# Transposing the keys and queries of batches 2 to 7 on VectorE in 32x32 blocks, in a fused top-k attention and feed-forward kernel

## The chip, the cores and the metric

The kernel runs on one core of a Trainium2 chip. The metric is the device time of one execution in microseconds (us). Three executions of the kernel before took 1657.47, 1657.69 and 1659.72 us; the median is 1657.69 us.

## The reference

Inputs are q, k and v of 8 batches, 8 heads, 576 tokens and 64 dimensions per head, all f32, and two weight matrices, 512x2048 and 2048x512, which arrive as 64-bit floats and are turned into f32 inside the kernel.

```
scores = scale * np.matmul(q, k.transpose(0, 1, 3, 2))
kth    = np.partition(scores, -32, axis=-1)[..., -32:-31]
scores = np.where(scores >= kth, scores, -1e9)
attn   = softmax(scores)                 # exp, divided by the row's sum
x      = matmul(attn, v), heads side by side   # 4608 rows of 512
h      = x @ w_in
out    = np.where(h > 0, h, exp(min(h, 0)) - 1) @ w_out
```

So each query row keeps its 32 largest of 576 scores; then 4608 rows go through a feed-forward block with the ELU function.

## The kernel before, in words

**Steps.** The attention is cut into 144 steps, 18 a batch. A step takes 128 queries of one pair of heads (the last 64 queries of a batch are shared out as steps that take two pairs of heads). Two heads of 64 dimensions fill the 128 partitions that a matmul sums over. The program is written out in one order by hand, step by step, and every engine runs its part of it in that order.

**What one step does.** TensorE makes the scores of two heads (`scores`, L322) two to three steps ahead; ScalarE copies them to SBUF (L342). VectorE finds the 32nd largest of each row in four rounds: `first_max` takes the eight largest of each head's row (L347), and `next_max` three times strikes the found ones out (`match_replace`, L353) and takes the next eight (L359). GpSimd makes the mask and applies it (L371 to L373), ScalarE takes the exponential and the row sums (L409). TensorE turns the result (`trans`, L449 and L467), ScalarE copies it out of PSUM (L454), and TensorE multiplies it with v (`attend`, L482). When all heads of a group of queries are done, `sums` has VectorE invert the row sums (L418 to L420) and sends them through DRAM to be spread over the partitions (L424, L436), and GpSimd scales the rows (`normalise`, L497).

**Keys and queries.** The scores need q and k with the head dimension on the partitions. For each batch and pair of heads, `load_qk` brings k and q into SBUF with tokens on the partitions (L228, L234), `transpose_qk` turns them: eight 128x128 and two 64-row transposes on TensorE into PSUM (L273, L281), and two ScalarE copies into a `kq` tile of 128 x 2 x 576 (L268). `keep_kq` writes the tile to DRAM (L296), and `load_kq` brings it back for each step that uses it (L302). `kq` tiles come from a ring of five (L95), the tiles that k and q are loaded into from a ring of two (L94). A table `turns` (L652) says at which step a pair is turned. There are four pairs of heads a batch, counted 0 to 31 over the batches: pairs 4 to 7 are turned in steps 2 to 5, pairs 8 to 12 in steps 7 to 11, and pairs 13 to 31 in every second step from 13 to 49. From step 6 on, steps with `transpose_qk` do it right after the scores (L721), and then issue the next pair's load. `load_kq` for steps n+3 and n+4 is issued at the head of an odd step n (L658).

**Feed-forward work.** Blocks of one to three groups of 128 rows become ready as groups are normalised. A block is a list of pieces: `hidden` (x times w_in, L517, then ELU on ScalarE and GpSimd, L531 to L534) and `project` (times w_out, L541, copied and stored, L550 and L553). `feed` is called twice a step and puts pieces into TensorE's order until the step's share is spent; even steps get two 0.3 parts of the share and odd steps two 0.7 parts. The share is what is left by the next due time, at most 6.0 in steps 0 to 71 and 7.2 after (L580); a unit of it stands for about a microsecond of TensorE. What is left after the last step is put out at the end.

**Queues.** All loads and stores but a few at the start are issued by SP, in program order; an issue whose data or buffer isn't ready holds up all behind it. In the first eight steps the weights are loaded and decoded, partly by VectorE.

Of the kernel before, what the change touches and what calls it, by code (L numbers as in the profile page):

```python
# [10 lines left out]
FP32 = mybir.dt.float32  # L11
# [50 lines left out]
def kernel(  # L62
# [9 lines left out]
    nc = tc.nc  # L72
    P = nc.NUM_PARTITIONS
    B, H, S, D = q.shape
    dm, dff = moe_w_in.shape[0], moe_w_in.shape[1] // 2
    J = S // P
    JP = J * P
    R = S - JP
    HS = S // 2
    NHP = H // 2  # L80
# [9 lines left out]
    def pool(name, bufs, **kw):  # L90
        return ctx.enter_context(tc.tile_pool(name=name, bufs=bufs, **kw))

    const = pool("const", 1)
    ldpool = pool("ld", 2)  # L94
    kqpool = pool("kq", 5)  # L95
# [115 lines left out]
    loaded, kqT, kept, vE = {}, {}, {}, {}  # L211

    def load_qk(b, hp):

        first = b == 0 and hp < 2
        aside = (b, hp) in ((0, 1), (0, 2))
        if aside:
            home = xtpool.tile([P, 2, NC * T // 2], FP32, tag="xT", name="kqin")
            home = home[:, :, 0 : (J + 1) * 2 * D].rearrange(
                "p n (j h d) -> p n j h d", j=J + 1, h=2  # L220
            )
        for n, (name, src) in enumerate((("k", k), ("q", q))):
            queue = nc.scalar if first and name == "q" else nc.sync
            if aside:
                t = home[:, n]
            else:
                t = ldpool.tile([P, J + 1, 2, D], FP32, tag="in", name=name + "in")
            queue.dma_start(  # L228
                t[:, 0:J, :, :],
                src[b, 2 * hp : 2 * hp + 2, 0:JP, :].rearrange(  # L230
                    "h (p j) d -> p j h d", j=J
                ),
            )
            queue.dma_start(  # L234
                t[0:R, J, :, :],
                src[b, 2 * hp : 2 * hp + 2, JP:S, :].rearrange("h p d -> p h d"),
            )
            loaded[b, hp, name] = t

    def load_v(b, hp):  # L240

# [56 lines left out]
    def load_kq(u):  # L298
        u.kq = {}
        for hp in u.hps:  # L300
            u.kq[hp] = kqpool.tile([P, 2, S], FP32, tag="kq", name="kq")
            nc.sync.dma_start(u.kq[hp][:], kept[u.g.b, hp][:])  # L302
# [271 lines left out]
    def feed(n, part):  # L574

        left = sum(piece[0] for piece in ffn)
        until = next(r for r in dues if r > n) - n
        share = min(left / until, 6.0 if n < NS // 2 else 7.2)  # L580

        work = 0.0
        for blk in order:
            mine = [piece[0] for piece in ffn if piece[3] is blk]
            work += sum(mine)
            late = work - 1.75 * 8 * blk.n
            if mine and late > 0 and blk.over is not None:
                share = max(share, late / max(blk.over.filled - n, 0.5))
        owed[0] = min(owed[0] + part * share, 8.0)
        while ffn and owed[0] > ffn[0][0] / 2 and ffn[0][2] < decoded[0]:  # L590
            t, piece = ffn.pop(0)[:2]
            piece()
            owed[0] -= t


    EARLY = 6
    sizes = {0: (1, 1, 1, 1, 1, 1, 1, 2), 2: (2, 2, 2, 3), B - 2: (3, 3, 2, 1)}
    steps, first, order = [], {}, []
    for b in range(B):
# [4 lines left out]
        for qt in (0, 1, 2, 3, 4) if b % 2 == 0 else (4, 0, 1, 2, 3):  # L604
            r0 = b * S + (JP if qt == J else qt)
            if qt == J:
# [3 lines left out]
                c0, n = slot * P + (b % 2) * R, R  # L610
                rows = slice(r0, r0 + R)
            else:
                blk, slot = places.pop(0)
                c0, n = slot * P, P
                rows = slice(r0, r0 + J * (P - 1) + 1, J)
            g = Tokens(b, qt, rows, blk, slice(c0, c0 + n))
# [11 lines left out]
    NS = len(steps)  # L628
    dues = [blk.ready for blk in order] + [NS + 5]

    def sums(u):
        u.summed = True
        invert(u.g)
# [3 lines left out]
        if place in ((2, 3, 4, 5, 6) if n in (4, 5) else (3, 4, 5, 6)):  # L637
            weight_slot()

    todo, turns = {}, {}  # L640

    def at(step, fn, *args):
        todo.setdefault(step, []).append((fn, args))
# [2 lines left out]


    for p, pair in enumerate(pairs):
        if p >= NHP:
            n = p - 2 if p < NHP + 4 else p - 1  # L650
            n = n if n < EARLY + 5 else EARLY + 5 + 2 * (n - EARLY - 5)
            turns[n] = pair  # L652
            at(n + 1, keep_kq, *pair)
        elif p >= 2:
            at(p - 1, keep_kq, *pair)

    for u in steps[EARLY + 2 :]:
        at(u.n // 2 * 2 - 3, load_kq, u)  # L658
    for hp in range(1, NHP):
        at(hp, load_v, 0, hp)  # L660
    for b in range(1, B):
# [5 lines left out]
    def load_next():  # L667
        if coming:
            load_qk(*coming.pop(0))

    with tc.manual_schedule():
        load_qk(0, 0)
        nc.scalar.activation(rec[:], rec[:], AF.Copy)
        for hp in (1, 2):
            load_qk(0, hp)
        load_weights(3)
        warm(16)
        for hp in range(2):
            transpose_qk(0, hp, shared=hp == 0)
            steps[hp].kq = {hp: kqT[0, hp]}  # L680
            scores(steps[hp], 0)
            scores(steps[hp], 1, nc.vector.tensor_copy if hp == 0 else nc.scalar.copy)
            if hp == 0:
                load_qk(0, 3)
        load_weights()
        load_v(0, 0)
        first_max(steps[0])
        weight_slot()
        weight_slot()
        for hp in range(2):  # L690
            keep_kq(0, hp)
        for n in range(NS + 4):
            early = n < EARLY
            now, last, done = (
                steps[n + d] if 0 <= n + d < NS else None for d in (0, -1, -2)
            )
            for fn, args in todo.pop(n, []):
                fn(*args)
            gone = None
            if early:  # L700
                if n + 2 < NHP:
                    transpose_qk(0, n + 2)
                ahead = steps[n + 2]
                ahead.kq = {hp: kqT[0, hp] for hp in ahead.hps}
                for half in range(2):
                    scores(ahead, half)
                if n < EARLY - 1:
                    warm(24)
            elif n % 2 == 0:

                for d in (2, 3):
                    if n + d < NS:
                        for half in range(2):
                            scores(steps[n + d], half)
                    if d == 2:
                        for u in steps[n - 4 : n - 2]:
                            if not u.attended:
                                attend(u)
                                gone = u
            if n in turns and not early:  # L720
                transpose_qk(*turns[n])  # L721
                load_next()
            if now and n > 0:
                first_max(now)
            if last and n > EARLY:
                biases(last, early)
                mask(last, 0)
            if early:
                decode(n, 0)
                feed(n, 0.5)  # L730
                if last:
                    exp(last, 0)
                    exp(last, 1)
                next_max(now, (n, 1))
                decode(n, 2)
                if last:
                    trans(last)
                feed(n, 0.5)
                if last and last.ends:
                    sums(last)  # L740
                next_max(now, (n, 3))
                decode(n, 4)
                if last:
                    attend(last)
                if n in turns:
                    transpose_qk(*turns[n])
                if n < EARLY - 1:
                    warm(24)
                next_max(now, (n, 5))
                if last and last.ends:  # L750
                    normalise(last.g)
                mask_early(now)
                decode(n, 6)
                if n >= NHP - 3:
                    load_next()
                continue
            decode(n, 0)
            feed(n, (0.3, 0.7)[n % 2])
            if now:
                next_max(now, (n, 1))  # L760
            decode(n, 2)
            if last:
                if n > EARLY:
                    mask(last, 1)
                exp(last, 0)
            if done and not done.turned:
                trans(done)
            if now:
                next_max(now, (n, 3))
            decode(n, 4)  # L770
            if gone and gone.ends:
                normalise(gone.g)
            feed(n, (0.3, 0.7)[n % 2])
            if now:
                next_max(now, (n, 5))
            decode(n, 6)
            if last:
                exp(last, 1)
            if done and done.ends and not done.summed:
                sums(done)  # L780
        while ffn:
            ffn.pop(0)[1]()

# [32 lines left out]
```

## Time and profile before

| what | us |
|---|---|
| median of three runs | 1657.69 |
| the profiled execution | 1660.85 |
| its span, first to last instruction | 1659.0 |
| TensorE busy | 1593.8 |
| VectorE busy | 1460.3 |
| GpSimd busy | 1141.9 |
| ScalarE busy | 925.5 |

The profile is of one execution. PE is TensorE's matmul and PEld its weight load, which overlaps it, DVE is VectorE, ACT is ScalarE, POOL is GpSimd, SP is SyncE, which only issues transfers. Matmuls are pipelined: a row's mean duration is longer than the distance from one matmul to the next, and the same holds, by less, for VectorE. An f32 product shows as two matmul records and a transpose as one. A group row reads: line, engine, operation, out<-in with shapes, count | busy us, mean ns of one | idle time of the engine before them and what ended it.

### The profile page before, as it was taken

What the parts mean: (1) busy time and instruction counts of PE and PEld (TensorE: products, weight loads), DVE (VectorE), ACT (ScalarE), POOL (GpSimd) and SP (SyncE); (2) the same over time, 40 slices, a digit from 0 to 9 for tenths busy, and PEclk for the clock granted to TensorE, in tenths of its full rate; (3) what the DMA queues carried; (4) which work ended last, traced back from release to release, by engine and by line L of the source; (5) the groups of instructions that cost most, each with busy time, mean ns of one, the idle gap of its engine ahead of it and who ended that gap; (6) DMA issues with size and microseconds to landing.
All of it is one profiled execution on the core that took longest, in us unless ns stands there. A gap on an engine that the chain in (4) does not pass through costs nothing.

```text
span 1659.0 us, 28820 instructions
## 1 busy us (share of the span) xinstructions
PE 1593.8 (96%) x10048; PEld 1074.0 (65%) x10048; DVE 1460.3 (88%) x3074; ACT 925.5 (56%) x1889; POOL 1141.9 (69%) x1456
## 2 busy tenths in 40 slices
PE   6868999999999999999999999999999999999999
PEld 5765877777776776757566566566565566566565
DVE  6999999999999999999999989979989989987000
ACT  5875565656666565646466475466466466455121
POOL 3677777777777786868678678668668668668021
PEclk8879999999999999999999999999999999999999
DMA  9864555444543513121212321221212322210000
GB/s 304 266 184 120 185 186 152 141 132 134 162 141 97 187 52 104 65 88 67 85 71 102 116 83 61 77 85 65 91 70 100 113 68 82 77 42 7 26 7 13
DMA packets 138962, 174.53 MB, mean 105 GB/s; under 512 B 94272, under 2 KB 102464, under 8 KB 138816
## 3 DMA queue, kind: packets, MB, share of 16 engines
q1 hardware_dynamic: 136448, 172.09, 32.3%
q8 instruction: 80, 1.31, 0.3%
q10 hardware_dynamic: 2368, 0.59, 0.2%
q14 instruction: 66, 0.54, 0.1%
HBM read 144.18 MB, written 28.46 MB: 104 GB/s over the span
## 4 chain that ended last, share of the span: by engine, by line
PE 59%; DVE 26%; POOL 5%; issue 4%; DMA 3%; ACT 2%; SPq 1%; POOLq 0%; ACTq 0%
PE ops L541 21%; PE hps L517 19%; DVE m L359 11%; DVE wk L353 11%; PE avps L482 6%; PE scps L322 6%; PE eps L449 4%; DVE m L347 2%; POOL sc L373 1%; POOL gT L534 1%; DMA kin<-in_k_dram 1%; DMA w_out<-in_moe_w_in_dram 1%; POOL wk L371 1%; PE qkps L273 1%; POOL wk L372 1%
## 5 line engine op out<-in xcount | busy, mean ns | idle before, releaser
L359 DVE MAX8 m<-wk 128x8 f32<-128x576 f32 x864 | 609.8, 748 | 0.0
L517 PE MATMUL hps<-xT,w_in 128*128 128x128 f32 (+2 forms) x2432 | 534.6, 375 | 10.4 <-ACT gT L532 5.7
L541 PE MATMUL ops<-w_out,gT 128*128 128x512 f32 x1152 | 519.6, 597 | 7.6 <-ACT osb L550 7.6
L517 PEld LDWEIGHTS hps<-xT,w_in 128*128 128x128 f32 x2432 | 385.0, 194 | 134.8 <-issue 18.5
L353 DVE MATCH_REPLACE8 wk<-m,wk 128x576 f32<-128x576 f32 x576 | 423.6, 744 | 0.0
L373 POOL TENSOR_TENSOR sc<-sc,wk 128x576 f32<-128x576 f32 x276 | 389.2, 1410 | 23.0
L541 PEld LDWEIGHTS ops<-w_out,gT 128*128 128x128 f32 x1152 | 209.9, 190 | 240.2 <-issue 214.2
L409 ACT ACTIVATE sc<-sc,neg 128x576 f32<-128x576 f32 x288 | 224.1, 778 | 229.6 <-POOL sc L373 228.8
L534 POOL TENSOR_TENSOR gT<-gT,n 128x384 f32<-128x384 f32 (+1 forms) x168 | 187.2, 1121 | 189.7 <-ACT n L533 187.0
L371 POOL TENSOR_SCALAR wk<-sc,nth 128x576 f32<-128x576 f32 x276 | 206.2, 747 | 26.9
L353 DVE MATCH_REPLACE8 wk<-m,sc 128x576 f32<-128x576 f32 x288 | 211.8, 744 | 0.0
L342 ACT COPY sc<-scps 128x576 f32<-128x576 f32 x287 | 168.9, 639 | 75.6 <-PE scps L322 73.6
L322 PE MATMUL scps<-kq 64*128 64x288 f32 (+3 forms) x1344 | 181.3, 419 | 23.7 <-ACT sc L342 9.9
L347 DVE MAX8 m<-sc 128x8 f32<-128x576 f32 x288 | 201.3, 741 | 0.3
L372 POOL TENSOR_SCALAR wk<-wk 128x576 f32<-128x576 f32 x276 | 184.0, 667 | 22.8
L454 ACT COPY et<-eps 128x1024 f32<-128x1024 f32 x144 | 144.5, 1004 | 96.3 <-PE eps L449 95.3
L482 PE MATMUL avps<-et,vE 128*64 128x128 f32 (+1 forms) x3200 | 176.3, 265 | 5.6 <-ACT et L454 3.3
L482 PEld LDWEIGHTS avps<-et,vE 128*64 128x64 f32 x3200 | 158.7, 137 | 32.1 <-issue 24.7
L449 PEld LDWEIGHTS eps<-ident,sc 128*128 128x128 f32 x1152 | 134.1, 141 | 54.2 <-issue 36.6
L322 PEld LDWEIGHTS scps<-kq 64*128 64x128 f32 (+1 forms) x1344 | 101.5, 175 | 93.3 <-issue 31.2
L449 PE MATMUL eps<-ident,sc 128*128 128x128 f32 x1152 | 151.1, 274 | 7.3 <-ACT sc L409 4.6
L531 ACT ACTIVATE n<-hps 128x384 f32<-128x384 f32 (+1 forms) x168 | 90.2, 537 | 114.0 <-PE hps L517 105.4
(71 smaller groups left out, 1001.3 us busy)
## 6 DMA issues: line engine op xcount, KB each, us to landing
kq<-kqd SPq DMA_DIRECT2D x152, 576.0 KB
kqd<-kq SPq DMA_DIRECT2D x32, 576.0 KB
rb<-recd SPq DMA_DIRECT2D x64, 128.0 KB
out_dram<-osb SPq DMA_DIRECT2D x32, 256.0 KB
kin<-in_k_dram SPq DMA_DIRECT2D x30, 256.0 KB
qin<-in_q_dram SPq DMA_DIRECT2D x29, 256.0 KB
w_out<-in_moe_w_in_dram SPq DMA_DIRECT2D x2, 2048.0 KB
vE<-in_v_dram SPq DMA_DIRECT2D x32, 128.0 KB
```

The costliest lines, as they stand in the source:

```text
L322: nc.tensor.matmul(ps[rows, j, at : at + keys.stop - keys.start], u.kq[hp][r, 1, q0 : q0 + g.ql], u.kq[hp][r, 0, keys], start=True, stop=True,
L347: nc.vector.max(u.m1[:, i, :], u.sc[:, i, :])
L353: nc.vector.match_replace(u.wk[:, i, :], u.m[:, i, :], u.cur[:, i, :], TAKEN)
L359: nc.vector.max(u.m[:, i, :], u.cur[:, i, :])
L371: nc.gpsimd.tensor_scalar(pen, s, u.nth[:, i : i + 1], 2.0**100, ALU.add, ALU.mult)
L373: nc.gpsimd.tensor_tensor(s, s, pen, ALU.add)
L409: nc.scalar.activation(s, s, AF.Exp, bias=u.neg[:, i : i + 1], scale=scale, accum_out=g.den[:, at : at + 1],)
L449: nc.tensor.transpose(ps[:, i, c * P : (c + 1) * P], e[:, k0 + c * P : k0 + (c + 1) * P], ident[:],)
L482: nc.tensor.matmul(g.av[r, hp, 0:ql], vE[g.b, hp][:, i, (c + i) % (J + 1), :], u.et[:, at, q0 : q0 + ql], start=(c == 0), stop=(c == J),)
L517: nc.tensor.matmul(ps[:, f % G, :], w_in[:, i, f * P : (f + 1) * P], blk.xT[:, i, 0:N], start=(i == 0), stop=(i == NC - 1),)
L534: nc.gpsimd.tensor_tensor(g, g, n, ALU.subtract)
L541: nc.tensor.matmul(blk.o[:], blk.gT[f // NG][:, f % NG, s * P : (s + 1) * P], w_out[:, f, :], start=(f == 0), stop=(f == NF - 1),)
```

## The change

Three things change.

1. `turns` keeps only pairs 4 to 7. Pairs 8 to 31 (batches 2 to 7) are loaded by a new `load_blocks` and turned by a new `transpose_blocks`, pair 8+j at the end of step 13+4j, the last in step 105. The new load puts 32 tokens by 32 dimensions blocks where VectorE's transpose wants them: partitions 32·part to 32·part+31 hold tokens, `part` names the head and half of its dimensions, and the free axis runs over token groups and 32 dimensions. It is four main and four remainder transfers for k, and as many for q, with runs of 32 f32. k is issued in step n-3 and q in step n-1, for a transpose in step n. One VectorE instruction of 128x576 turns k and one turns q, straight into the `kq` tile.
2. `load_kq` for steps n+4 and n+5 is issued in even step n, behind the scores.
3. The cap on the feed-forward share is 6.6 in place of 6.0 in steps 0 to 71.

```diff
+    def load_blocks(b, hp, name):
+        t = ldpool.tile([P, J + 1, 2, D], FP32, tag="in", name=name + "bl")
+        t = t[:].rearrange("p j h d -> p (j h d)")[:, 0:S]
+        main = t[:, 0:JP].rearrange("p (c g d) -> p c g d", c=J, d=32)
+        rem = t[:, JP:S].rearrange("p (g d) -> p g d", d=32)
+        for part in range(4):
+            rows = slice(32 * part, 32 * part + 32)
+            h, d0 = 2 * hp + part // 2, part % 2 * 32
+            src = (k if name == "k" else q)[b, h, :, d0 : d0 + 32]
+            nc.sync.dma_start(
+                main[rows], src[0:JP].rearrange("(g i c) d -> i c g d", i=32, c=J)
+            )
+            nc.sync.dma_start(
+                rem[rows], src[JP:S].rearrange("(g i) d -> i g d", i=32)
+            )
+        loaded[b, hp, name] = t
+
+    def transpose_blocks(b, hp):
+        t = kqT[b, hp] = kqpool.tile([P, 2, S], FP32, tag="kq", name="kq")
+        for n, name in enumerate("kq"):
+            nc.vector.transpose(t[:, n, :], loaded.pop((b, hp, name)))
...
-        share = min(left / until, 6.0 if n < NS // 2 else 7.2)
+        share = min(left / until, 6.6 if n < NS // 2 else 7.2)
...
     for p, pair in enumerate(pairs):
-        if p >= NHP:
-            n = p - 2 if p < NHP + 4 else p - 1
-            n = n if n < EARLY + 5 else EARLY + 5 + 2 * (n - EARLY - 5)
-            turns[n] = pair
+        if p >= 2 * NHP:
+            n = EARLY + 7 + 4 * (p - 2 * NHP)
+            blocks_at[n] = pair
+            behind.setdefault(n - 3, []).append((load_blocks, (*pair, "k")))
+            behind.setdefault(n - 1, []).append((load_blocks, (*pair, "q")))
             at(n + 1, keep_kq, *pair)
+        elif p >= NHP:
+            turns[p - 2] = pair
+            at(p - 1, keep_kq, *pair)
...
-    for u in steps[EARLY + 2 :]:
-        at(u.n // 2 * 2 - 3, load_kq, u)
+    for u in steps[EARLY + 2 : EARLY + 4]:
+        at(EARLY - 1, load_kq, u)
...
-            if n in turns and not early:
-                transpose_qk(*turns[n])
-                load_next()
+                for u in steps[n + 4 : n + 6]:
+                    load_kq(u)
+                for fn, args in behind.pop(n, []):
+                    fn(*args)
...
+            if n in blocks_at:
+                transpose_blocks(*blocks_at[n])
```

(EARLY is 6, NHP is 4. The two `for` loops stand inside the branch for even steps, behind the scores; the last two lines stand at the very end of a step, behind `sums`.)

More of the change, by code (lines that the diff above doesn't have):

```diff
@@ L638, in decode @@
             weight_slot()
-    todo, turns = {}, {}
+    todo, turns, blocks_at, behind = {}, {}, {}, {}
     def at(step, fn, *args):
```

## The prediction

> **What bounds the kernel now.** I read the page's busy shares first, then busy time by stretch, VectorE's waits, and the timelines of the places that the change touches. The page has two engines near full.
>
> ```profile
> PE 1593.8 (96%) x10048; PEld 1074.0 (65%) x10048; DVE 1460.3 (88%) x3074; ACT 925.5 (56%) x1889; POOL 1141.9 (69%) x1456
> ```
>
> A mean over stages doesn't say which is the limit. The windows do; the columns are PE, PEld, DVE, ACT, POOL busy with instruction counts, then the granted clock, DMA share and GB/s. I cut at the start of step 13 (188.34 us; a step's start is its first L347), of step 80 (847.13), and at the end of VectorE's work (1523).
>
> ```profile
> 0.00:188.34 188.34, 150.71 (x1075) 122.63 (x1076) 171.23 (x340) 122.63 (x225) 118.99 (x144) 0.88 0.74 224
> 188.34:847.13 658.79, 647.02 (x4587) 467.28 (x4586) 657.33 (x1399) 391.71 (x787) 500.55 (x644) 1.00 0.38 120
> 847.13:1523.00 675.87, 666.25 (x3860) 404.57 (x3860) 631.20 (x1335) 382.20 (x824) 497.36 (x646) 1.00 0.22 76
> 1523.00:1659.00 136.00, 129.82 (x534) 79.54 (x530) 0.59 (x3) 28.94 (x56) 25.00 (x24) 0.99 0.04 14
> ```
>
> From 188 to 847 us VectorE is busy 657.3 of 658.8: it sets the pace there. From 847 on it has 44.7 us idle, which end on the mask (below), and the mask waits in GpSimd's order behind feed-forward pieces that wait for TensorE: there TensorE sets the pace. After 1523 us only TensorE works, on what is left of the feed-forward. So an extra VectorE microsecond counts in full up to about step 80, and from there to the end TensorE's amount of work counts.
>
> ```profile
> DVE wk L353 <- POOL sc L373: 46.2, 16, 7.6
> ```
>
> [...] The trace has a transpose of 32 columns only (211 ns, below), and other 576-element VectorE instructions at 743 ns; neither shows the rate of a long f32 transpose. [...]
>
> **The change part by part.** *TensorE's transposes go.* One undisturbed pair in TensorE's timeline:
>
> ```profile
> 188.15 0.60 PE L273 MATMUL qkps<-ident,kin 128*128 128x128 f32 x4
> 188.59 0.60 PE L273 MATMUL qkps<-ident,qin 128*128 128x128 f32 x4
> 189.12 0.27 PE L281 MATMUL qkps<-ident,kin 64*128 64x64 f32 x1
> 189.23 0.22 PE L281 MATMUL qkps<-ident,qin 64*128 64x64 f32 x1
> 189.38 3.39 PE L517 MATMUL hps<-xT,w_in 128*128 128x128 f32 x28
> ```
>
> From 188.15 to the next work at 189.38 is 1.23 us. 24 pairs free 24 x 1.23 = 29.5 us of TensorE, all before step 50, where VectorE sets the pace: alone worth nothing in that stage. ScalarE loses 24 copies of 1009 ns and 24 of 275, 31 us; it is 56% busy, so zero.
>
> *VectorE's transposes come.* 48 of 128x576. The nearest priced neighbours are these, in VectorE's timeline at the end of a step:
>
> ```profile
> 512.24 0.95 DVE L418 TENSOR_SCALAR den<-den 128x8 f32<-128x8 f32 x1
> 513.23 0.20 DVE L419 RECIPROCAL rec<-den 128x8 f32<-128x8 f32 x1
> 513.47 0.21 DVE L420 STREAM_TRANSPOSE recT<-rec 128x32 f32<-128x32 f32 x1
> 513.60 1.38 DVE L347 MAX8 m<-sc 128x8 f32<-128x576 f32 x2
> 514.90 0.07 DVE L353 MATCH_VALUE_LOAD wk<-m,sc 128x8 f32 x1
> ```
>
> 32 columns take 0.21, and the next instruction starts 0.08 before that ends[...]. So 0.78 long and 0.70 from start to start; a pair 1.40 us. Floor: two MAX8 of 576, 1.30 (513.60 to 514.90). [...] I take 1.40: the 0.21 us for 32 columns is no more than a RECIPROCAL of 8. Pairs 8 to 22 fall in steps 13 to 69: 15 x 1.40 = **+21.0 us** on the path. The other nine fall in steps 73 to 105, where TensorE takes over as the limit; 12.6 us stand against 44.7 us of idle VectorE time in that half. The idle time is not where they are in every case, so I charge **+1**; without any cover they cost 12.6.
>
> *Share 6.6.* Counting matmuls in both programs up to the first scores of step 72: before, 208 products of `project` and 224 of `hidden` at 256 columns; after, 224 and 256. So 16 and 32 products move from the TensorE-bound half into the VectorE-bound one. Their price is from the tail's timeline, two records to a product:
>
> ```profile
> 1570.67 27.79 PE L517 MATMUL hps<-xT,w_in 128*128 128x256 f32 x128
> 1598.29 13.90 PE L541 MATMUL ops<-w_out,gT 128*128 128x512 f32 x32
> ```
>
> 27.62/128 = 0.216 and 13.9/32 = 0.434 a record: 32 x 0.434 + 64 x 0.216 = 13.9 + 13.8 = **-27.7 us** from 769 us on. This needs room on TensorE in steps 13 to 71: the 19 pairs turned there free 23.4, and VectorE's 21.0 lengthen the stage, against 27.7 more work. It fits. Without the freed time it would not.
>
> *The start.* Five pairs leave steps 7 to 11. In step 12 VectorE waits 3.07 us for a mask that stood behind late TensorE work:
>
> ```profile
> 180.00 0.09 DVE L353 MATCH_VALUE_LOAD wk<-m,sc 128x8 f32 x1 [3.07 <-POOL sc L373]
> ```
>
> The higher share refills part of the room; I take **-2** (0 to -4).
>
> *Transfers.* A pair's load was 2368 packets; in a 4 us window of the trace that holds just these they took 65.0% of 16 engines, 0.65 x 4 = 2.6 us. The new pair has 4608 runs of half the size, so at most 5.1 us at the old price per packet, but in four steps (39 us) and not in two. SP's issues, on the same window's timeline:
>
> ```profile
> 460.70 0.62 SPq L228 DMA_DIRECT2D kin<-in_k_dram  x1
> 461.36 0.73 SPq L234 DMA_DIRECT2D kin<-in_k_dram  x1
> ```
>
> 0.66 us each: 16 a pair, 10.6 us in 39, where 4 took 2.6 in 19. q goes out in step n-1 behind the two `kq` loads (1.3 us): 1.3 + 5.3 + about 4 to land makes 11 us from the step's head, and VectorE wants it at the end of step n, 19 us on. Hidden with 8 us to spare; what hides it is two steps of MAX8 and MATCH_REPLACE8. k has two steps more. If a stall came, VectorE's next `first_max` and, a step later, mask and exponential would be late. Stores of finished rows are queued on SP ahead of these loads and wait for TensorE, which eats into the margin only where TensorE lags, in the second half. `keep_kq` moves with its pair; the copy in DRAM is read eight steps later or more. `load_kq` a step sooner removes no visible wait (no TensorE wait on these loads is among the listed ones): zero; the ring slots it takes were last read by scores of the same or earlier even steps.
>
> The new VectorE waits are for k's and q's transfers and for a free `kq` slot (last read by scores that stand at the head of the step before, or earlier). Queued behind them are the next step's L347, and on it everything of that step.
>
> **Sum:** +21.0 + 1 - 27.7 - 2 = -7.7 us on the profile's span of 1659.0, 1651.3. The profiled execution is 3.2 us over the median; the same difference on the median gives 1650.0.
>
> **Rivals.** (A) *The f32 transpose streams at half rate.* At 2.6 a pair, 15 pairs cost 39.0 and the later nine 23, of which I charge 4: 39 + 4 - 27.7 - 2 = +13, 1671. For it: no long transpose is in the trace. [...] It turns the sign from (27.7 + 2 - 1)/15 = 1.9 us a pair. (B) *No cover in the second half:* VectorE's later transposes delay masks and so open gaps on TensorE; +12.6 in place of +1 gives +3.9 at worst, about half of it -1.9: 1656. For it: from step 73 to 105 both engines are nearly full. (C) *The block loads come late:* each stall s counts 15 times; from s = 0.5 us the gain is gone; 2 us gives 1680. Against: the 8 us of margin. (D) *More is gained:* ScalarE's copies and their PSUM tiles no longer stand between scores and transposes, the start gains its 4 us and the transposes cost the floor: 19.5 - 27.7 - 4 - 3 = -15, 1643. That the change does nothing is excluded by the instruction order, where 240 TensorE transposes are gone.
>
> **How the numbers follow.** My forecast (1644 to 1654) has 0.50, D 0.14, B 0.14, A 0.12, C 0.08, others slower 0.02. A measurement here tells about 0.2%, 3.3 us, from no change. Faster: forecast and D, 0.64. Same: B, 0.14. Slower: 0.22. The range reaches from D's middle at 1641 to near A's time, 1668; C and most of A lie beyond.
>
> **What would show it.** Steps without inversion in the first half stay 9.64 us from L347 to L347, and every fourth is longer by 1.4; transposes of 128x576 last 0.78; VectorE has no idle time on k or q transfers; step 72 starts near 769 + 21 - 2 = 788 us; TensorE's tail after VectorE's end is shorter. Wrong if transposes last over 0.95, if VectorE waits for `in_q_dram`, or if TensorE has gaps after step 72 that were not there before.

## The result, and the profile after

The changed kernel takes 1663.82 us (median of 7 executions, 1661.80 to 1664.41) against 1659.72 us (7, 1657.47 to 1661.20) for the kernel before on the same chip: ratio 1.0025, 95% interval 1.0013 to 1.0037. It is slower by some 4 us, where 7.7 us faster was forecast. The time lies inside the range that the prediction gave, 1641 to 1668 us, and on the other side of no change than forecast. Of the runs below, one execution of the last (the mix with the reserve) took 3263.77 us, twice its others, and is left out of its median.

The page of the changed kernel, busy shares:

```profile
PE 1567.4 (94%) x9808; PEld 1047.5 (63%) x9808; DVE 1494.2 (90%) x3122; ACT 897.7 (54%) x1841; POOL 1143.7 (69%) x1456
```

TensorE lost 26.4 us of busy time, VectorE gained 33.9. The stretches below are cut at the starts of steps 14, 72, 81 and 143 (the first L347, now L373, of the step in VectorE's timeline). First the kernel before, then the changed one; columns are PE, PEld, DVE, ACT, POOL, then clock, DMA share and GB/s.

```profile
0.00:199.46 199.46, 161.83 (x1144) 130.19 (x1148) 182.28 (x364) 129.55 (x239) 128.08 (x158) 0.89 0.71 215
199.46:768.94 569.48, 558.75 (x4110) 409.63 (x4102) 568.23 (x1209) 340.51 (x682) 432.06 (x553) 1.00 0.40 126
768.94:856.77 87.83, 86.79 (x491) 56.68 (x492) 87.69 (x188) 49.62 (x104) 65.11 (x85) 1.00 0.22 74
856.77:1512.97 656.20, 646.58 (x3738) 391.98 (x3737) 611.83 (x1296) 371.14 (x799) 482.15 (x627) 1.00 0.23 78
1512.97:1659.00 146.03, 139.85 (x576) 85.54 (x574) 10.31 (x24) 34.66 (x69) 34.50 (x35) 0.99 0.04 13
```

```profile
0.00:199.89 199.89, 156.22 (x1152) 124.29 (x1154) 182.37 (x366) 124.49 (x232) 129.58 (x162) 0.90 0.59 182
199.89:791.97 592.08, 562.97 (x3964) 407.58 (x3958) 587.90 (x1238) 324.55 (x658) 436.72 (x554) 0.99 0.40 114
791.97:886.64 94.67, 88.37 (x475) 54.54 (x472) 90.83 (x191) 55.81 (x121) 71.85 (x93) 0.96 0.37 104
886.64:1539.28 652.64, 642.02 (x3711) 386.23 (x3711) 622.75 (x1309) 363.35 (x777) 476.98 (x620) 1.00 0.30 91
1539.28:1662.60 123.32, 117.79 (x520) 74.87 (x518) 10.31 (x24) 29.55 (x56) 28.55 (x29) 0.99 0.04 13
```

Differences, in order: start to step 14 +0.4; steps 14 to 71 +22.6; steps 72 to 80 +6.8; steps 81 to 142 -3.6; step 143 and the tail -22.7. They sum to the 3.6 us between the two spans.

What a turned pair costs, in VectorE's timeline of the changed kernel:

```profile
320.37 0.20 DVE L445 RECIPROCAL rec<-den 128x8 f32<-128x8 f32 x1
320.61 0.21 DVE L446 STREAM_TRANSPOSE recT<-rec 128x32 f32<-128x32 f32 x1
320.98 0.78 DVE L264 STREAM_TRANSPOSE kq<-kbl 128x576 f32<-128x576 f32 x1 [0.16 <-issue]
321.68 0.73 DVE L264 STREAM_TRANSPOSE kq<-qbl 128x576 f32<-128x576 f32 x1
322.34 1.38 DVE L373 MAX8 m<-sc 128x8 f32<-128x576 f32 x2
```

The prediction's 0.78 us a transpose, which no line of the kernel before showed, came out at 0.78 and 0.73 us. But the first doesn't start 0.13 us after the short transpose of the row sums, as L347 did before (513.47 to 513.60); it starts 0.37 after, 0.16 of it idle. From 320.61 + 0.13 to 322.34 the pair costs 1.60 us; 14 pairs between steps 14 and 71 make 22.4 of the 22.6 us. VectorE's waits of the whole run show no k or q transfer among the causes; the columns are us in total, times, longest us:

```profile
DVE wk L379 <- POOL sc L399: 35.0, 19, 3.9
DVE kq L264 <- issue: 2.8, 15, 0.4
DVE kq L264 <- PE scps L348: 0.9, 5, 0.2
```

### The profile page after: what moved, and what is told of

Read it like the earlier page. It is cut to its first block, busy times and chain, and to the rows that moved or that the text cites. A ratio compares the mean times of both kernels' runs of the same rounds, so it can differ in the third digit from the quotient of the medians.

```text
span 1662.6 us, 28736 instructions
## 1 busy us (share of the span) xinstructions
PE 1567.4 (94%) x9808; PEld 1047.5 (63%) x9808; DVE 1494.2 (90%) x3122; ACT 897.7 (54%) x1841; POOL 1143.7 (69%) x1456
## 3 DMA queue, kind: packets, MB, share of 16 engines
q1 hardware_dynamic: 196352, 172.11, 34.8%
## 4 chain that ended last, share of the span: by engine, by line
PE 53%; DVE 29%; POOL 6%; issue 5%; ACT 4%; DMA 2%; SPq 1%; DVEq 0%; POOLq 0%; ACTq 0%
PE ops L567 18%; PE hps L543 18%; DVE m L385 13%; DVE wk L379 12%; PE avps L508 6%; PE scps L348 6%; PE eps L475 4%; DVE m L373 2%; POOL sc L399 2%; POOL wk L397 1%; POOL gT L560 1%; POOL wk L398 1%; DVE kq L264 1%; PE idle L318 1%; ACT sc L435 1%
## 5 line engine op out<-in xcount | busy, mean ns | idle before, releaser
L373 DVE MAX8 m<-sc 128x8 f32<-128x576 f32 x288 | 200.9, 738 | 0.1
L391 POOL TENSOR_SCALAR nth<-m 128x2 f32<-128x2 f32 x138 | 30.2, 219 | 194.6 <-DVE m L385 146.8
```

Source lines behind the costliest of these rows:

```text
L373: nc.vector.max(u.m1[:, i, :], u.sc[:, i, :])
```

## The experiments

Medians below stand beside the kernel before on the same chip (1658.7 to 1659.2 us in the three sets); the changed kernel's is 1663.82. They come from several chips, and with the intervals given a difference between two of them is uncertain by some 2 to 3 us. Four runs first took the parts of my sum one at a time. The letters P, B and D of the theories in the expectations are those defined there, not the letters of the prediction's rivals.

**The cap alone undone.** On the changed kernel:

```diff
-        share = min(left / until, 6.6 if n < NS // 2 else 7.2)
+        share = min(left / until, 6.0 if n < NS // 2 else 7.2)
```

> The changed kernel with the cap on the feed-forward share back at 6.0 in steps 0 to 71; VectorE still turns the keys and queries. Theory P (the prediction's: from step 72 on TensorE's amount of work alone counts): the 28 us of feed-forward that went forward come back behind step 72 in full, 1664 + 28 = 1692 us. Theory B (from step 72 to 143 VectorE and TensorE set the pace in turn, so only what leaves the tail counts in full): the tail had lost 22.7 us, so 1664 + 22 = 1686, with the time from step 72 to 143 about as before.

Measured: 1682.13 us, ratio to the kernel before 1.0132 (1.0117 to 1.0147). So 6.6 is worth 18.3 us in the changed kernel; both theories had put it higher, P by ten and B by four. The windows of its steps 72 to 80, 81 to 142, and 143 to the end:

```profile
790.35:881.76 91.41, 90.38 (x502) 58.75 (x503) 90.58 (x191) 52.90 (x111) 68.16 (x89) 1.00 0.33 97
881.76:1534.39 652.63, 642.98 (x3727) 389.36 (x3726) 621.12 (x1310) 367.74 (x792) 478.89 (x624) 1.00 0.29 91
1534.39:1680.50 146.11, 139.85 (x576) 85.42 (x574) 10.31 (x24) 34.66 (x69) 34.77 (x35) 0.99 0.04 13
```

From the start of step 72 to the end it takes 1680.50 - 790.35 = 890.15 us; the kernel before takes 1659.00 - 768.94 = 890.06. The changed kernel takes 870.63. What comes after step 72 depends on the cap, and 6.6 takes 19.5 us off it, not 27.7.

**The cap alone made.** On the kernel before, 6.6 in place of 6.0 and nothing else.

> The kernel before with nothing changed but the cap, 6.6 in place of 6.0; TensorE still turns everything. If TensorE has no room in steps 13 to 71 while it turns the pairs, as the prediction said, VectorE begins to wait there and little is won: 1655 to 1662 us. If it has room (its matmuls at their dense spacing fill only some 550 of 581 us there), the step lengths stay at 9.64 and the tail falls by about 22: 1636 to 1640 us, and then the transposes on VectorE were not needed for the gain.

Measured: 1655.87 us, ratio 0.9974 (0.9964 to 0.9985): faster than either kernel. After step 72 it takes 1652.10 - 783.41 = 868.69, the same gain. But steps 14 to 71 are 17.5 us longer than before:

```profile
196.41:783.41 587.00, 581.72 (x4175) 425.27 (x4171) 570.83 (x1210) 348.88 (x698) 437.45 (x557) 1.00 0.39 121
```

VectorE is idle for 16.2 us of them, and TensorE busy for 581.72 of the 587.00: it has no room for both the transposes and the greater share, as the prediction said. So the change buys off this 17.5 us with 22.6 us of VectorE time.

**The later nine pairs left out, and all 24.** In the changed kernel, with 23 or 8 as the first pair that is left out:

```diff
-            at(n + 1, keep_kq, *pair)
+            if p < 23:
+                at(n + 1, keep_kq, *pair)
...
-                transpose_blocks(*blocks_at[n])
+                b, hp = blocks_at[n]
+                if b * NHP + hp < 23:
+                    transpose_blocks(b, hp)
+                else:
+                    kept[b, hp] = kept[1, hp]
```

> The changed kernel without the last nine pairs' transposes and their copies to DRAM (pairs 23 to 31, steps 73 to 105): their loads stay, and the steps that need them read pairs of batch 1 instead, so that part of the scores is not computed from the right keys. Theory P (TensorE paces there and idle VectorE time covers them): 1662 to 1664 us. Theory B (they are paid in full on VectorE, 1.62 us a pair): 1664 - 14.6 = 1649 us.

> The same with all 24 pairs left out (no VectorE transposes of keys and queries, no copies of them to DRAM; loads stay; steps of batches 2 to 7 read batch 1's pairs). The first 15 pairs cost 15 x 1.62 = 24 us in steps 13 to 71. Theory P: 1664 - 24 = 1640 us, if TensorE has the room for its feed-forward share in the shorter steps. Theory B: 1664 - 38.9 = 1625 us, less what TensorE then can't follow, so 1625 to 1632.

Measured: 1663.87 us (1.0028, 1.0016 to 1.0039) and 1639.71 us (0.9882, 0.9865 to 0.9898). The nine pairs behind step 72 cost nothing that can be told from noise, where 14.6 us would have been the full price; the 15 before it cost 1663.82 - 1639.71 = 24.1 us, 1.61 each. Theory P holds for the pairs. Without the nine pairs, steps 72 to 80 take as long as with them (94.67):

```profile
792.35:887.41 95.06, 88.32 (x475) 54.57 (x472) 88.11 (x187) 55.76 (x121) 71.78 (x93) 0.96 0.33 91
```

With no pair turned, the stretch from step 72 on takes 1637.20 - 768.30 = 868.90 us, again that of the cap 6.6. Its steps 72 to 80, and 81 to 142:

```profile
768.30:861.26 92.96, 88.17 (x481) 54.73 (x478) 88.00 (x187) 55.68 (x121) 71.88 (x93) 0.98 0.36 95
861.26:1513.90 652.64, 642.03 (x3711) 386.21 (x3711) 613.35 (x1295) 363.13 (x777) 477.29 (x620) 1.00 0.28 85
```

Steps 72 to 80 are 5.1 us longer than the kernel before's 87.83 although VectorE turns nothing here, and VectorE is idle for 5.0 of them. That is where part of the share's gain went.

**The empty queue.** In the changed kernel, TensorE's timeline in step 74 and then VectorE's in step 77:

```profile
813.21 1.88 PE L567 MATMUL ops<-w_out,gT 128*128 128x512 f32 x4
820.26 9.00 PE L543 MATMUL hps<-xT,w_in 128*128 128x384 f32 x20 [5.17 <-POOL xT L523]
842.39 6.62 PE L543 MATMUL hps<-xT,w_in 128*128 128x384 f32 x20
```

```profile
847.15 0.09 DVE L379 MATCH_VALUE_LOAD wk<-m,sc 128x8 f32 x1 [3.32 <-POOL sc L399]
```

At 6.6 the pieces of the old blocks run out before the new block is scaled; TensorE waits 5.17 us for it, is late afterwards, and VectorE waits for a mask. The wait costs more than its length: the 20 records behind it take 9.00 us, and 20 of the same kind later 6.62. The granted clock (the third number from the end) was lower in the wait and behind it, and 1.00 again from 825 us on:

```profile
815.00:820.00 5.00, 0.09 (x1) 0.00 (x0) 5.00 (x11) 3.29 (x7) 4.14 (x5) 0.81 0.55 204
820.00:825.00 5.00, 4.74 (x8) 2.59 (x9) 5.00 (x11) 0.00 (x0) 1.71 (x5) 0.51 0.42 95
```

To test whether the empty queue is the cause, the share was worked out so as to leave a reserve:

```diff
         left = sum(piece[0] for piece in ffn)
+        left = max(left - 8.0, 0.0) if 60 <= n < 74 else left
```

> The changed kernel, where in steps 60 to 73 the share is worked out from what is left less 8 units, so that the queue of feed-forward pieces isn't empty when the block of step 74 becomes ready. Theory D (the empty queue makes TensorE wait some 5 us in step 74, and VectorE pays for it in step 77): both waits go, steps 72 to 80 get about 4 us shorter (94.6 to 90 us), and the tail, which gets 5 units more, about 5 us longer: 1662 to 1665 in all. If the queue is not the cause, VectorE's wait near step 77 stays, and the tail's 5 us make it 1669.

Measured: 1661.52 us, ratio 1.0017 (1.0010 to 1.0024). Steps 72 to 80, then 81 to 142, then the rest:

```profile
791.34:883.33 91.99, 86.41 (x473) 53.03 (x470) 91.51 (x192) 53.73 (x116) 69.57 (x91) 1.00 0.34 96
883.33:1530.68 647.35, 639.59 (x3711) 386.54 (x3710) 619.95 (x1309) 363.28 (x781) 478.12 (x622) 1.00 0.30 91
1530.68:1660.20 129.52, 124.05 (x535) 77.72 (x533) 10.31 (x24) 30.14 (x57) 28.52 (x29) 1.00 0.04 15
```

VectorE's idle time in steps 72 to 80 falls from 94.67 - 90.83 = 3.8 us to 0.5, those steps by 2.7 us, the ones behind them by 5.3, and the tail gets 6.2 of it back. TensorE's wait in step 74 is gone, and the clock of steps 72 to 80 is 1.00 in place of 0.96. So the empty queue was the cause of the waits. Filling it earns little, 2.3 us by the medians, which is no more than their uncertainty: the reserve is work that then isn't done early.

**The first transpose's wait.** In the changed kernel the two transposes go ahead of the row sums' inversion:

```diff
+            if n in blocks_at:
+                transpose_blocks(*blocks_at[n])
             if done and done.ends and not done.summed:
                 sums(done)
-            if n in blocks_at:
-                transpose_blocks(*blocks_at[n])
```

> The changed kernel with the two VectorE transposes ahead of the inversion of the row sums and not behind it. If the 0.16 to 0.19 us ahead of the first transpose are VectorE's sequencer working through four waits behind a 0.21 us instruction, a 0.75 us MAX8 in front hides them: a pair falls from 1.61 to 1.42 us, 15 x 0.19 = 2.9 us, 1661 us. If they are a transfer's lateness, they stay: 1664. A risk: the inversion and with it GpSimd's scaling come 1.4 us later.

Measured: 1661.00 us, ratio 1.0009 (1.0000 to 1.0017).

```profile
316.45 1.41 DVE L385 MAX8 m<-wk 128x8 f32<-128x576 f32 x2
317.78 0.76 DVE L264 STREAM_TRANSPOSE kq<-kbl 128x576 f32<-128x576 f32 x1
318.46 0.73 DVE L264 STREAM_TRANSPOSE kq<-qbl 128x576 f32<-128x576 f32 x1
319.12 0.13 DVE L444 TENSOR_SCALAR den<-den 128x8 f32<-128x8 f32 x1
```

The idle time is gone and a pair costs 319.12 - 317.78 = 1.34 us, 0.26 less. The transposes start earlier here with the same loads, so a late transfer is not the cause. The changed kernel's trace has semaphore waits at the transposes' line, four ahead of nearly every one of the 48:

```profile
L264 DVEq EVENT_SEMAPHORE  x186: 21/50/50, 198.1 to 1150.6; - x186
```

(21/50/50 are the shortest, median and longest in ns.) In this run none of the 46 transposes that start between 200 and 1200 us has idle time ahead of it. That the 0.16 us went into these waits, where only an instruction of 0.21 us stood in front and not a MAX8 of 0.74, fits both runs; no run isolates it. The median falls by 2.8 us, as expected, though that is no more than its uncertainty.

**The earlier reload.** I had put it at zero. First alone on the kernel before, then undone in the changed kernel (the second diff):

```diff
-    for u in steps[EARLY + 2 :]:
-        at(u.n // 2 * 2 - 3, load_kq, u)
+    for u in steps[EARLY + 2 : EARLY + 4]:
+        at(EARLY - 1, load_kq, u)
...
+                for u in steps[n + 4 : n + 6]:
+                    load_kq(u)
             if n in turns and not early:
```

> The kernel before with nothing changed but the reload of kq tiles one step sooner, behind the scores of an even step. No wait on these loads is to be seen in the kernel before, so every theory here says no change: 1657 to 1662 us, and within 0.2% of the kernel before.

```diff
-    for u in steps[EARLY + 2 : EARLY + 4]:
-        at(EARLY - 1, load_kq, u)
+    for u in steps[EARLY + 2 :]:
+        at(u.n // 2 * 2 - 3, load_kq, u)
...
-                for u in steps[n + 4 : n + 6]:
-                    load_kq(u)
```

> The changed kernel with the reload of kq tiles put back to the head of the odd steps, as in the kernel before. If the earlier reload only hurts where TensorE turns a pair in nearly every step and waits for its k (steps 7 to 11 of the kernel before), it is without effect in the changed kernel, which turns none there: 1662 to 1666 us. If it costs the changed kernel the 4 us that it cost the kernel before, 1659 to 1660 us.

Measured: 1663.34 us alone (1.0028, 1.0019 to 1.0038), and 1671.52 us undone (1.0084, 1.0070 to 1.0098). Both expectations failed. Alone, the reloads stand ahead of the load of a k that TensorE is about to turn, in the dense turns of steps 7 to 11; that wait was 0.82 us in the kernel before, and VectorE's wait for a mask in step 12 grows with it from 3.07 to 6.53:

```profile
169.28 1.09 PE L273 MATMUL qkps<-ident,kin 128*128 128x128 f32 x4 [4.71 <-DMA kin<-in_k_dram]
```

Undone in the changed kernel, the block loads stand ahead of the reloads. SP's timeline while VectorE is in step 39, the end of ten issues of v and eight of k, and then TensorE's wait:

```profile
457.79 0.58 SPq L252 DMA_DIRECT2D kbl<-in_k_dram  x1
458.41 0.63 SPq L255 DMA_DIRECT2D kbl<-in_k_dram  x1
459.45 0.36 SPq L579 DMA_DIRECT2D out_dram<-osb  x1
459.86 0.95 SPq L328 DMA_DIRECT2D kq<-kqd  x2
460.85 0.60 SPq L252 DMA_DIRECT2D qbl<-in_q_dram  x1
```

```profile
466.19 2.29 PE L348 MATMUL scps<-kq 64*128 64x288 f32 x8 [6.60 <-DMA kq<-kqd]
```

TensorE waits 6.60 us for a reload that was queued behind those eighteen, and VectorE 8.14 in step 41. The earlier reload is what keeps the sixteen new issues a pair from hurting; it is not an optional part of the change.

**A version that beats both.** If turning is free on VectorE behind step 72 and dear before it, and TensorE can bear half of the pairs at cap 6.6, then each should do its own. On the changed kernel:

```diff
-        if p >= 2 * NHP:
-            n = EARLY + 7 + 4 * (p - 2 * NHP)
+        if p >= 21:
+            n = 73 + 4 * (p - 21)
...
-            turns[p - 2] = pair
-            at(p - 1, keep_kq, *pair)
+            n = p - 2 if p < 2 * NHP else 13 + 4 * (p - 2 * NHP)
+            turns[n] = pair
+            at(n + 1, keep_kq, *pair)
...
+            if n in turns and not early:
+                transpose_qk(*turns[n])
+                load_next()
             if now and n > 0:
                 first_max(now)
```

> A mix meant to beat both kernels: cap 6.6; pairs 8 to 20 turned by TensorE (load_qk, transpose_qk) in every fourth step from 13 to 61, pairs 21 to 31 by VectorE in blocks in every fourth step from 73 to 113. If VectorE's transposes are free behind step 72 and cost 1.61 us each before it, and 13 pairs at 1.23 us on TensorE over steps 13 to 61 can be borne, the step lengths in the first half go back to 9.64 and 10.2, and 15 x 1.61 = 24 us come off the changed kernel: 1640 us, up to 1645 if TensorE is short of some of the 16 us. If TensorE has no room for them at cap 6.6, VectorE waits and it gives 1650 to 1656, like the kernel before at cap 6.6.

> The mix (pairs 8 to 20 turned by TensorE to step 61, pairs 21 to 31 by VectorE from step 73) with the reserve of 8 units in steps 60 to 73. The reserve took 2.3 us off the changed kernel; the mix lost less to the empty queue (0.9 us of idle VectorE in steps 72 to 80 against 3.8), so it gains less here: 1643 to 1647 us, no difference from the mix without it.

Measured: 1645.12 us, ratio to the kernel before 0.9915 (0.9899 to 0.9931); with the reserve 1643.89 us (three executions), 0.9914 (0.9899 to 0.9929), no difference. Steps 14 to 71 of the first:

```profile
198.11:777.23 579.12, 573.76 (x4114) 418.66 (x4110) 571.49 (x1209) 342.27 (x685) 437.40 (x557) 1.00 0.34 111
```

They are 9.6 us longer than before, 13.0 shorter than in the changed kernel; VectorE's idle time there is 7.6 us, 6.3 of it waiting for a mask. That TensorE is still a little short of room would fit, but was not tested.

## Why the prediction was wrong, step by step

| step of the sum | predicted | measured | by |
|---|---|---|---|
| 15 pairs on VectorE up to step 69 | +21.0 | +24.1 | all 24 left out |
| nine pairs behind step 72 | +1 | 0 | later nine left out |
| share 6.6 | -27.7 | -18.3 | cap back at 6.0 |
| the start, first pair taken out | -2 | -1.2 | profiles: +0.4 to step 14, less 1.6; within their spread |
| sum | -7.7 | +4.6 | medians: +4.1 |

The terms come from different sets and are uncertain by 2 to 3 us each; that their sum comes so near to the medians' +4.1 is in part luck.

**What bounds the kernel** was read right for VectorE: its time counted in full before step 72 and not at all behind it. That the freed TensorE time is worth nothing in itself was right too: at cap 6.0 the changed kernel is 22.9 us slower than the kernel before, about the price of its transposes.

**The step that failed is the share.** "16 and 32 products move from the TensorE-bound half into the VectorE-bound one" was counted right, and their price was nearly right: from step 72 to the end TensorE's busy time falls from 873.22 to 848.18 us, by 25.0. What failed is that all of the -27.7 was taken off the time, as if TensorE worked without a gap from 769 us on. Its idle time there grew by 5.6 us, and the time fell by 19.4. The windows say where. The tail got 22.7 us shorter. Steps 72 to 142 got none of the other 5.0: they take 744.03 us in the kernel before, 744.04 in the changed kernel at cap 6.0, 745.60 at 6.6 with no pair turned, and 747.31 in the changed kernel.

Two things stand behind that. The higher cap emptied the queue in step 74, as the run with the reserve shows; at cap 6.0 there is no such gap (TensorE is busy for 90.38 of the 91.41 us of steps 72 to 80), and the kernel before at 6.6 has one of 2.84 us. The 5.17 us gap is also one of the prediction's own signs of being wrong, a gap of TensorE behind step 72 that was not there before. And I had put the turning point at step 80, but counted the gain from step 72: in steps 72 to 80 of the kernel before VectorE was busy 87.69 of 87.83 us, so that work which TensorE is spared there can hardly free anything. This second part is argued from the busy times; no run isolates it.

The turned pairs have no part in the loss: at cap 6.0 they make steps 72 to 80 longer by 3.6 us and steps 81 to 142 shorter by as much.

**The start** held two waits that I had not foreseen. In step 10 TensorE idles for 6.93 us in place of 1.94. This comes with the pairs that left steps 7 to 11, not with the cap: the wait is there at cap 6.0 without these pairs, and stays short at 6.6 with them. The lines are from the kernel before, the changed kernel, the changed kernel at 6.0, and the kernel before at 6.6:

```profile
164.60 0.71 PE L517 MATMUL hps<-xT,w_in 128*128 128x128 f32 x4 [1.94 <-POOL xT L497]
163.60 8.44 PE L543 MATMUL hps<-xT,w_in 128*128 128x128 f32 x48 [6.93 <-POOL xT L523]
166.71 5.91 PE L543 MATMUL hps<-xT,w_in 128*128 128x128 f32 x36 [6.28 <-POOL xT L523]
161.64 2.04 PE L517 MATMUL hps<-xT,w_in 128*128 128x128 f32 x12 [1.99 <-POOL xT L497]
```

The 3.07 us of VectorE in step 12, which I had looked for to go, shrink to 0.62, and a wait of 3.24 comes in step 13 in their place. That one goes with the cap: it is 3.25 us in the kernel before at 6.6, and absent in both kernels at 6.0. How much the start changed as a whole can't be told: three runs that are the same program up to there begin step 14 between 198.96 and 200.82 us, and the kernel before at 199.46.

**The pair's price** was mis-sized by 0.2 us. The 1.40 us were my estimate: the kernel before has no VectorE transpose of more than 32 columns, so its trace showed no price for a long one. The transposes came out as estimated; the gap ahead of the first, 0.37 us from start to start where 0.13 stood before, was not counted. With it the 15 pairs are 24.1. This alone doesn't turn the sign: -7.7 + 3.1 = -4.6. The share alone does: -7.7 + 9.4 = +1.7.

**The transfers** were hidden, as forecast: no wait of VectorE on k or q. 59904 more packets at the same bytes took the main queue from 32.3% to 34.8% of 16 engines, some 43 us per engine over the run: 1.8 us a pair, where 5.1 - 2.6 = 2.5 had been allowed. (The prediction's "same window" is a slip: its packets are from 345 to 349 us, its issue lines from 460 us.) But "`load_kq` a step sooner: zero" was wrong about its role; without it the changed kernel is 7.7 us slower still.

**Rivals.** A (2.6 us a pair, an assumption that no trace had shown) and C (late blocks) did not happen: a transpose took 0.73 to 0.78 us, and VectorE waited for no block. B had the cost in the wrong place: the later pairs are covered. D did not happen (its time is given as 1643 us in its sum and as 1641 in the range). The slower side was reached by no mechanism that I listed, but by the gain's being a third smaller than counted.

Left open: what holds up the mask in steps 14 to 71 of the mix; why the reserve made steps 81 to 142 shorter by 5.3 us, which its expectation didn't have; and how much of the missing 5.0 us is owed to VectorE's pace in steps 72 to 80.

## What to carry to other kernels

When work is moved out of a stretch to shorten it, count only what leaves the steps that its engine really paces, step by step and not by halves: here 22.7 us in the tail counted and the other 5.0 did not. A queue that is drained faster also runs empty sooner, and then the engine waits for the next supply. Before an engine is relieved, price the relief by itself: here a greater share on the old kernel won more (3.4 us) than the relief and the share together, and in the version that beats both each transpose stands on the engine that had room for it at that time.

## What the runs showed of the hardware

- A VectorE transpose of 128x576 f32 took 0.73 to 0.78 us, 0.66 to 0.70 from start to start. It has 544 columns more than the one of 128x32 f32, which took 0.21 us, and took 0.52 to 0.57 longer: about 1 ns a column.
- In the changed kernel a VectorE transpose with four semaphore waits of 21 to 50 ns ahead of it came after 0.16 us of idle time, 0.37 us from start to start, behind an instruction of 0.21 us. Put behind a MAX8 of 0.74 us, it came with no idle time.
- SP took 0.58 to 0.63 us to issue each of eight block loads, 64 KB and 8 KB alike, and 5.2 us for all (453.82 to 459.0 in the run with the reload put back). Behind these and ten issues of v, a reload came 6.60 us late for TensorE.
- Behind TensorE's wait of 5.17 us in step 74 of the changed kernel the granted clock was 0.51 for 5 us (0.81 in the wait), and 20 records took 9.00 us, where 20 of the same kind took 6.62 at clock 1.00.
